# A gated linear recurrence and a two-layer network on one core: the decay sums' last rows turned by VectorE, the last output in two halves, another order of loads and work

## The chip, the cores and the metric

The kernel runs on one core of a Trainium2 chip. A core has five engines with a queue each: PE (TensorE, matmuls; its weight loads are shown apart as PEld), DVE (VectorE), ACT (ScalarE), POOL (GpSimd) and SP (SyncE, which issues the DMA transfers here). The engines work at the same time and wait for each other by semaphores. PSUM, into which PE writes, has eight banks of 128 partitions x 512 f32 values. The metric is device time in microseconds (us): the median of several executions, and beside it one execution that the hardware profiler recorded.

## The reference, cut to what matters

```python
# q, k, v, f_logit: (4 batches, 8 heads, 768 steps, 48), f32
f = 1.0 / (1.0 + np.exp(-f_logit))
for t in range(S):
    state = f[:, :, t, :, None] * state + np.einsum('bhd,bhe->bhde', k[:, :, t], v[:, :, t])
    y[:, :, t] = np.einsum('bhd,bhde->bhe', q[:, :, t], state)
x = y.transpose(0, 2, 1, 3).reshape(B * S, H * D)     # 3072 tokens x 384
h = x @ w_in                                          # 384 -> 2048
g = np.maximum(0.01 * h, h)
out = g @ w_out                                       # 2048 -> 384
```

Each head keeps a 48 x 48 state that decays with a gate for each of its rows; the outputs go through a two-layer network with a leaky relu.

## The kernel before

**Chunks.** The 768 steps are cut into six chunks of 128. Inside a chunk the recurrence is a masked product: with the running sum of -log f over the chunk, k is multiplied by exp(sum) and q by exp(-sum), the scores k q are masked to the lower triangle and multiplied with v. What came before the chunk enters through the state, and the state is carried to the chunk's end by a factor exp(-sum of the whole chunk), the tile `end`: one value for each row of each head's state, that is, for each pair of heads one column of 128 partitions (head one in partitions 0 to 47, head two in 64 to 111).

**Units.** Work comes in twelve units of 256 tokens. Units 0 to 3 are one batch each with its first two chunks ("paired"); units 4 to 11 are one chunk (2 to 5) of two batches. Since a chunk of a batch needs the state of the chunk before, unit 6 needs what unit 4 leaves, and so on.

**Steps.** The kernel is one long string, `order` (L537 to L602), whose words are run one after the other when the program is built. A word is a step, a unit, a half or group of it, an engine choice where there is one, and after "@" the PSUM banks that it writes. Each engine runs its own instructions in the string's order; the string therefore sets every queue. `manual_schedule` leaves this order as it is, and waits between engines are put in by the framework: where two engines touch one PSUM bank, the later one in the string waits for the earlier.

The steps of a unit, in the order in which data pass through them:
- Lf, Lk, Lq, Lv: loads, on SP (WI, WO: the pieces of the two weight matrices; w_in comes in two pieces of 256 columns and three of 512, w_out in four; cw casts a block of them to bf16 on the engine named last: 0 DVE, 1 ACT, 2 POOL).
- ge, gl (L231, L243): ACT makes log(1 + exp(-f_logit)).
- cs (L252 to L263): PE makes the running sums with a triangular matrix, one matmul of 384 columns for each half of units 4 to 11 (L260). In units 4 to 9 four matmuls of one column follow (L263): for a pair of heads p they multiply the pair's 128 columns with a column of ones, which gives the last row of the sums, turned into a column of 128 partitions.
- dec (L271, L272, L277): ACT takes exp(sum) into `em`, exp(-sum) into `at`, and of the four turned columns exp(-sum) into `end`.
- k, q (L283, DVE or POOL), v (L288 to L297, POOL): scaling and casts to bf16.
- tk, tq and ck, cq (L316, L331): transposes on PE and copies out of PSUM; in units 6 to 11 xk and xq, DMA transposes, instead.
- sc (L352, L359) scores, mk (L369, L373) masks on DVE, mx and ms (L390) the products with v and with the state, xt (L450, L452) the copy of x.
- pt (L463, L468) the chunk's k v, sf (L478, L480) its addition to the state on DVE, sb (L485, L488) the state's factor and its copy to bf16 on POOL.
- up (L496): the first layer for 256 of the 2048 inner values, 6 matmuls of 256 columns (eight groups for a unit); pr (L501): the leaky relu on ACT; dn (L508): a quarter of the second layer for 128 tokens, 4 matmuls of 384 columns; ob (L517 ACT, L519 DVE): the copy of the finished 128 x 384 outputs; st (L523): the store.
- id (L203): matmuls on constants that nothing reads, between the true ones at the start.

The first layer of a unit can start when x is there, so units' steps are laid between the up and dn groups of units before. The last words of the string are `dn_11_1_3 ob_11_0_1 st_11_0 ob_11_1_0 st_11_1`.

Of the kernel before, what the change touches and what calls it, by code (L numbers as in the profile page):

```python
# [15 lines left out]
def kernel(  # L16
# [228 lines left out]
    def cs(j, a, bank):  # L245
# [15 lines left out]
        if chunk(j, a) < NCH - 1:  # L261
            for p in range(P2):
                nc.tensor.matmul(t[:, H * D + p:H * D + p + 1], lf[:, a, 2 * p:2 * p + 2, :], ones_col,  # L263
                                 start=True, stop=True)
# [4 lines left out]
    def dec(j, a):
        t = banks[st[j]["cs", a]]  # L270
        nc.scalar.activation(ems[j % 2][:, a], t[:, 0:H * D], AF.Exp, scale=1.0)  # L271
        nc.scalar.activation(ats[j % 2][:, a], t[:, 0:H * D], AF.Exp, scale=-1.0)  # L272
        if paired(j):
            nc.scalar.activation(end_of(j)[:, :, 2 * a:2 * a + 2].rearrange("t i p -> t p i"),
                                 t[:, 384:388].rearrange("t (p i) -> t p i", i=2), AF.Exp, scale=-1.0)
        elif chunk(j, a) < NCH - 1:
            nc.scalar.activation(end_of(j)[:, a], t[:, H * D:H * D + P2], AF.Exp, scale=-1.0)  # L277
# [263 lines left out]
    id_8@2 sc_0_1@0.1 mk_0_0_1 mk_0_1_1 id_5@4 pt_0_2@2.3 WI_3 ge_1_0 mk_0_1_0 ge_1_1 gl_1_0 sf_0_0 id_8@6
    mx_0_2@4.5 gl_1_1 Lk_2_2 cs_1_0@6 sb_0_0 xt_0_0_1 cs_1_1@7 dec_1_0 WI_4 sf_0_1 ms_0 k_1_0_1 dec_1_1 q_1_0_0
    Lq_2_2 k_1_1_0 v_1_1 id_13@0 tk_1_0@1 xt_0_1_1 tq_1_0@0 q_1_1_0 tk_1_1@2 ck_1_0_1 v_1_0 cq_1_0_0 Lv_2_2
    tq_1_1@4 ck_1_1_1 sc_1_0@3.6 cq_1_1_0 cw_0_0_2 pt_1_2@7.5 mk_1_0_0 sc_1_1@1.0 sb_0_1 cw_0_1_0 up_0_0@2
    ge_2_0 mk_1_1_1 up_0_1@4 ge_2_1 mk_1_0_1 gl_2_0 pr_0_0 cs_2_0@3 mk_1_1_0 gl_2_1 sf_1_0 dec_2_0 cw_0_2_2
    mx_1_2@0.6 cw_0_3_0 cs_2_1@2 sb_1_0 pr_0_1 dec_2_1 xt_1_0_0 WO_0 id_5@7 up_0_2@1 sf_1_1 cw_0_4_2 cw_0_5_1
    up_0_3@7 sb_1_1 pr_0_2 ms_1 WO_1 up_0_5@3 pr_0_3 xt_1_1_0 Lf_3_2 up_0_4@4 k_2_0_0 Lk_3_2 k_2_1_1 pr_0_5
    up_1_2@0 pr_0_4 tk_2_1@2 pr_1_2 up_1_5@5 ck_2_1_1 cw_0_6_0 up_1_3@1 pr_1_5 tk_2_0@6 cw_0_7_0 pr_1_3 up_1_0@7
    ck_2_0_1 up_1_1@3 q_2_1_0 WO_2 pr_1_0 q_2_0_0 up_0_7@4 v_2_0 pr_1_1 tq_2_1@0 pr_0_7 tq_2_0@2 v_2_1 cq_2_1_0
    up_1_6@5 cq_2_0_1 sc_2_1@1.6 pr_1_6 cw_1_0_2 cw_1_1_0 sc_2_0@7.3 pt_2_2@4.0 up_1_4@2 mk_2_1_1 WO_3 mk_2_1_0  # L550
    Lq_3_2 dn_0_1_0@5 pr_1_4 Lv_3_2 mk_2_0_0 dn_0_0_0@6 cw_1_3_1 Lf_4_0 sf_2_0 up_1_7@1 Lk_4_0 ge_3_0 mk_2_0_1
    sb_2_0 up_0_6@2 ge_3_1 Lq_4_0 gl_3_0 cw_1_2_0 mx_2_2@7.4 gl_3_1 pr_0_6 cs_3_0@3 sf_2_1 Lv_4_0 xt_2_0_1 ms_2
    dn_0_1_1 sb_2_1 dec_3_0 k_3_0_0 dn_0_0_1 xt_2_1_1 pr_1_7 Lf_4_1 tk_3_0@2 cw_1_4_2 cw_1_5_0 up_2_6@0 up_2_4@7
    ck_3_0_0 pr_2_6 dn_0_1_2 pr_2_4 Lk_4_1 cw_1_6_2 cw_1_7_0 up_2_3@3 up_2_5@4 pr_2_3 Lq_4_1 q_3_0_1 up_2_7@1
    pr_2_5 up_2_0@2 Lv_4_1 v_3_0 pr_2_7 dn_0_0_2 pr_2_0 v_3_1 Lf_5_0 cs_3_1@0 dn_0_0_3 dec_3_1 Lk_5_0 up_2_1@7
    k_3_1_1 ob_0_0_0 Lq_5_0 up_2_2@3 pr_2_1 q_3_1_1 dn_1_1_0@4 pr_2_2 st_0_0 tk_3_1@1 tq_3_0@2 ck_3_1_0 tq_3_1@0
    Lv_5_0 ge_4_2 dn_0_1_3 cq_3_0_0 cq_3_1_0 sc_3_0@6.7 gl_4_2 ob_0_1_0 sc_3_1@3.1 pt_3_2@2.0 mk_3_0_1 Lf_5_1
    dn_2_1_0@5 mk_3_1_1 cs_4_0@7 mk_3_1_0 Lk_5_1 dn_1_1_1 dec_4_0 mk_3_0_0 cs_4_1@1 Lq_5_1 v_4_2 dn_1_1_2 sf_3_0
    dec_4_1 dn_2_1_1 k_4_2_0 Lv_5_1 sb_3_0 dn_1_1_3 q_4_2_0 Lf_6_0 dn_2_1_2 ob_1_1_1 sf_3_1 pt_4_0@3 tq_4_0@7
    Lk_6_0 tk_4_1@6 sf_4_0 dn_2_1_3 sb_3_1 Lq_6_0 ck_4_1_0 tk_4_0@2 cq_4_0_0 dn_1_0_0@1 Lv_6_0 ck_4_0_0 sb_4_0  # L560
    tq_4_1@4 dn_1_0_1 cq_4_1_1 Lf_6_1 mx_3_2@0.3 ge_5_2 sc_4_2@6.7.2.4 Lk_6_1 xt_3_0_0 gl_5_2 ms_3 mk_4_0_0
    dn_1_0_2 Lq_6_1 xt_3_1_0 cs_5_0@0 dn_1_0_3 mk_4_1_1 st_0_1 dec_5_0 v_5_2 mk_4_1_0 up_3_3@6 ob_1_0_1 mk_4_0_1
    cs_5_1@3 pr_3_3 up_3_1@4 st_1_0 dec_5_1 dn_2_0_0@0 k_5_2_1 pr_3_1 st_1_1 up_3_2@2 dn_2_0_1 pr_3_2 Lv_6_1
    q_5_2_1 up_3_4@1 Lf_7_0 pt_5_1@7 up_3_0@6 pr_3_4 sf_5_1 up_3_6@3 Lk_7_0 ge_6_2 sb_5_1 tq_5_1@4 pr_3_0
    tq_5_0@2 Lq_7_0 cq_5_1_0 up_3_5@1 gl_6_2 cq_5_0_0 dn_2_0_2 Lv_7_0 pr_3_6 cs_6_0@7 pr_3_5 Lf_7_1 cs_6_1@6
    ob_2_1_1 tk_5_0@4 Lk_7_1 tk_5_1@2 dec_6_1 ck_5_0_0 pt_5_0@3 st_2_1 dn_3_1_0@1 ck_5_1_0 sf_5_0 dec_6_0
    dn_2_0_3 Lq_7_1 v_6_2 dn_3_1_1 ob_2_0_1 Lv_7_1 pt_4_1@5 q_6_2_1 dn_3_0_0@4 sf_4_1 dn_3_1_2 Lf_8_0 dn_3_0_1
    sb_4_1 sc_5_2@2.6.3.7 st_2_0 mx_4_2@0.5 mk_5_0_0 k_6_2_1 mk_5_1_1 Lk_8_0 dn_3_0_2 xt_4_0_1 mk_5_0_1 xt_4_1_1
    up_3_7@2 xq_6 sb_5_0 ge_7_2 mk_5_1_0 up_4_2@7 pr_3_7 pt_6_1@0 xk_6 up_4_5@5 gl_7_2 sf_6_1 dn_3_0_3 pr_4_2
    sb_6_1 Lq_8_0 pr_4_5 dn_3_1_3 ob_3_0_0 Lv_8_0 pt_6_0@6 cs_7_0@3 ob_3_1_0 v_7_2 st_3_0 up_4_7@2 dec_7_0  # L570
    sf_6_0 up_4_6@0 Lf_8_1 sb_6_0 pr_4_7 Lk_8_1 up_4_0@7 pr_4_6 cs_7_1@5 pr_4_0 Lq_8_1 up_4_1@4 dec_7_1 up_4_4@1
    k_7_2_1 pr_4_1 up_4_3@6 pr_4_4 st_3_1 dn_4_1_0@3 pr_4_3 q_7_2_1 dn_4_0_0@2 pt_7_0@0 pt_7_1@7 dn_4_0_1 sf_7_0
    sf_7_1 mx_5_2@5.4 xk_7 sc_6_2@1.6.0.7 xt_5_0_1 sb_7_0 xq_7 dn_4_0_2 xt_5_1_1 mk_6_0_0 up_5_4@5 mk_6_0_1
    sb_7_1 Lv_8_1 dn_4_0_3 mk_6_1_1 pr_5_4 Lf_9_0 mk_6_1_0 up_5_6@4 ge_8_2 Lk_9_0 up_5_5@1 ob_4_0_1 Lq_9_0
    gl_8_2 up_5_0@6 pr_5_5 Lv_9_0 dn_4_1_1 pr_5_0 Lf_9_1 up_5_2@7 pr_5_6 up_5_7@5 pr_5_2 up_5_3@0 pr_5_7 Lk_9_1
    up_5_1@2 pr_5_3 dn_4_1_2 pr_5_1 cs_8_1@1 dn_5_1_0@6 Lq_9_1 dec_8_1 dn_4_1_3 dn_5_1_1 ob_4_1_0 Lv_9_1 v_8_2
    sc_7_2@4.7.5.0 dn_5_0_0@2 Lf_10_0 mk_7_0_0 dn_5_1_2 mk_7_1_1 st_4_1 dn_5_0_1 mk_7_0_1 mk_7_1_0 dn_5_1_3
    Lk_10_0 dn_5_0_2 ob_5_1_0 Lq_10_0 cs_8_0@1 dn_5_0_3 dec_8_0 Lv_10_0 mx_6_2@3.4 k_8_2_0 ge_9_2 q_8_2_1
    Lf_10_1 mx_7_2@0.7 ob_5_0_0 xt_6_0_1 xt_6_1_0 gl_9_2 pt_8_0@5 xk_8 xt_7_0_0 pt_8_1@6 up_6_4@1 xt_7_1_1
    sf_8_0 v_9_2 up_6_1@2 xq_8 pr_6_4 sf_8_1 up_6_2@3 pr_6_1 sb_8_0 up_6_0@4 Lk_10_1 pr_6_2 st_4_0 up_7_0@0  # L580
    pr_6_0 sb_8_1 Lq_10_1 cs_9_0@7 pr_7_0 dn_6_1_0@5 Lv_10_1 dec_9_0 up_6_3@1 up_6_6@6 pr_6_3 cs_9_1@2 st_5_0
    pr_6_6 up_6_5@3 dec_9_1 dn_6_1_1 st_5_1 k_9_2_1 pr_6_5 up_7_1@4 ge_10_2 up_7_4@0 pr_7_1 q_9_2_1 up_6_7@7
    xk_9 gl_10_2 pt_9_0@1 up_7_7@6 pr_6_7 sf_9_0 pr_7_4 dn_6_0_0@2 sb_9_0 xq_9 pr_7_7 up_7_5@3 dn_6_0_1 pr_7_5
    Lf_11_0 cs_10_1@4 up_7_6@7 Lk_11_0 dec_10_1 dn_6_1_2 Lq_11_0 pr_7_6 sc_8_2@1.0.6.3 Lv_11_0 v_10_2 dn_6_1_3
    mk_8_0_0 Lf_11_1 up_7_3@4 mk_8_0_1 Lk_11_1 ob_6_1_1 dn_6_0_2 mk_8_1_0 pr_7_3 mk_8_1_1 dn_7_0_0@7 dn_6_0_3
# [51 lines left out]
```

## Time and profile before

| | |
|---|---|
| median of 3 executions | 180.60 us (180.38 to 181.57) |
| profiled execution | 180.96 us |
| its span, first to last instruction | 179.0 us |
| granted clock of TensorE | 1.000 |
| read from and written to memory | 25.17 MB, 4.72 MB |

The page lists each engine's busy time with its share of the span, then 40 equal slices of the span (a digit is the busy share in tenths), the chain of work that ended last, and groups of instructions: line, engine, operation, output<-input, count, then busy us and mean ns of one, then the engine's idle us ahead of them with what ended it. The larger groups beside those that the prediction shows:

```profile
L496 PE MATMUL ps<-xT,w_in 128*128 128x256 bf16 x576 | 71.0, 273 | 1.0 <-issue 1.0
L508 PE MATMUL ps<-w_out,gT 128*128 128x384 bf16 x384 | 72.0, 326 | 0.0
...
L373 DVE TENSOR_TENSOR wm<-ps,ut 128x512 bf16<-128x512 f32 x32 | 20.0, 683 | 20.0 <-PE ps L359 12.2
...
L271 ACT ACTIVATE em<-ps 128x384 bf16<-128x384 f32 x24 | 11.9, 495 | 10.9 <-PE ps L263 7.3
```

The matmuls are pipelined, so a matmul's duration (273, 326 ns) holds its way through the array; from the start of one to the start of the next it is 109 ns for 256 columns and 162 ns for 384.

### The profile page before, as it was taken

The numbers are of one execution on the slowest core, as the hardware profiler recorded it, in microseconds if no ns is written. First come the engines' busy times: TensorE is split into PE (matmuls) and PEld (weight loads), VectorE is DVE, ScalarE is ACT, GpSimd is POOL, SyncE is SP. The second block draws the span as 40 slices with busy tenths as digits, with TensorE's granted clock in tenths as the row PEclk, the third lists the DMA queues.
The fourth block names the chain that finished last, engine by engine and source line by source line (L and its number), as shares of the span: only waits on it lengthen the run. The fifth ranks groups of instructions, "written<-read, shape, count | busy, mean of one in ns | idle before, by whom it ended". The sixth has DMA issues, their size and how long they took to land.

```text
span 179.0 us, 5623 instructions
## 1 busy us (share of the span) xinstructions
PE 171.8 (96%) x2326; PEld 130.9 (73%) x2326; DVE 81.4 (45%) x167; ACT 113.4 (63%) x234; POOL 74.4 (42%) x143
## 2 busy tenths in 40 slices
PE   7898979999999999999999999999999999999992
...
DVE  7878953961398714560711770142056065120001
...
GB/s 138 286 313 339 380 320 379 355 322 194 204 206 156 176 263 180 238 199 207 209 171 217 165 229 165 221 149 220 208 77 92 161 4 44 48 44 4 0 88 88
DMA packets 102105, 33.39 MB, mean 186 GB/s; under 512 B 96448, under 2 KB 100288, under 8 KB 102080
## 3 DMA queue, kind: packets, MB, share of 16 engines
...
q8 instruction: 18, 0.29, 0.6%
q14 instruction: 7, 0.06, 0.1%
HBM read 25.17 MB, written 4.72 MB: 167 GB/s over the span
## 4 chain that ended last, share of the span: by engine, by line
PE 87%; DVE 4%; DMA 2%; issue 2%; SPq 1%; POOL 1%; ACT 0%; DVEq 0%; ACTq 0%; POOLq 0%
PE ps L508 36%; PE ps L496 35%; PE ps L390 6%; DVE wm L369 3%; PE ps L359 2%; PE ps L316 2%; DMA q_raw<-in_q_dram 2%; PE ps L260 1%; SPq L154 1%; PE ps L468 1%; PE ps L352 1%; POOL qh L283 1%; PE ps L263 1%; PE ps L463 0%; DVE kh L283 0%
## 5 line engine op out<-in xcount | busy, mean ns | idle before, releaser
L496 PE MATMUL ps<-xT,w_in 128*128 128x256 bf16 x576 | 71.0, 273 | 1.0 <-issue 1.0
L508 PE MATMUL ps<-w_out,gT 128*128 128x384 bf16 x384 | 72.0, 326 | 0.0
L501 ACT ACTIVATE gT<-ps 128x512 bf16<-128x512 f32 x96 | 56.5, 603 | 20.6 <-PE ps L496 18.5
L496 PEld LDWEIGHTS <-w_in 128*128 128x128 bf16 x576 | 60.3, 110 | 6.8 <-issue 1.2
L508 PEld LDWEIGHTS <-gT 128*128 128x128 bf16 x384 | 35.7, 98 | 19.1
L373 DVE TENSOR_TENSOR wm<-ps,ut 128x512 bf16<-128x512 f32 x32 | 20.0, 683 | 20.0 <-PE ps L359 12.2
L519 DVE COPY osb<-ps 128x384 f32<-128x384 f32 x11 | 6.1, 557 | 35.7 <-PE ps L508 35.6
L480 DVE TENSOR_TENSOR sf<-sf,ps 64x192 f32<-64x192 f32 x32 | 11.2, 351 | 20.9 <-PE ps L468 8.5
L271 ACT ACTIVATE em<-ps 128x384 bf16<-128x384 f32 x24 | 11.9, 495 | 10.9 <-PE ps L263 7.3
L488 POOL CAST sb<-sf 64x192 bf16<-64x192 f32 x40 | 14.4, 361 | 10.0 <-DVE sf L478 7.7
L283 POOL TENSOR_TENSOR qh<-q_raw,at 128x768 bf16<-128x768 f32 (+1 forms) x9 | 13.6, 1509 | 10.8 <-ACT end L277 8.9
L283 POOL TENSOR_TENSOR kh<-k_raw,em 128x768 bf16<-128x768 f32 (+1 forms) x8 | 11.0, 1373 | 14.6 <-ACT em L271 11.2
L288 POOL CAST vb<-v_raw 128x384 bf16<-128x384 f32 (+1 forms) x16 | 11.3, 708 | 12.1 <-PE ps L496 4.7
L450 ACT CAST xT<-ps 128x384 bf16<-128x384 f32 x14 | 7.0, 526 | 11.4 <-PE ps L390 11.4
L517 ACT COPY osb<-ps 128x384 f32<-128x384 f32 x13 | 6.3, 482 | 11.5 <-PE ps L508 11.3
L231 ACT ACTIVATE e<-f_raw 128x384 f32<-128x384 f32 (+1 forms) x16 | 10.6, 684 | 2.4 <-DMA f_raw<-in_f_logit_dram 2.4
L272 ACT ACTIVATE at<-ps 128x384 bf16<-128x384 f32 x24 | 11.9, 497 | 0.0
L485 POOL TENSOR_TENSOR sf<-sf,end 128x192 f32<-128x192 f32 x16 | 8.4, 527 | 6.5 <-DVE sf L480 6.1
L243 ACT ACTIVATE lf<-e 128x384 bf16<-128x384 f32 (+1 forms) x16 | 10.7, 683 | 0.1
L369 DVE TENSOR_TENSOR wm<-ps,pair_mask 128x512 bf16<-128x512 f32 x16 | 10.1, 683 | 1.4 <-PE ps L352 1.3
L203 PE MATMUL ps<-warm 128*128 128x512 bf16 (+2 forms) x22 | 7.3, 452 | 1.1 <-DVE warm L82 1.1
L452 DVE CAST xT<-ps 128x384 bf16<-128x384 f32 x10 | 5.5, 568 | 4.9 <-PE ps L390 3.6
...
## 6 DMA issues: line engine op xcount, KB each, us to landing
...
```

Source lines behind the costliest of these rows:

```text
L271: nc.scalar.activation(ems[j % 2][:, a], t[:, 0:H * D], AF.Exp, scale=1.0)
L272: nc.scalar.activation(ats[j % 2][:, a], t[:, 0:H * D], AF.Exp, scale=-1.0)
L283: eng.tensor_mul(heads(j, to[j % NR], a)[:, :, :, 0:D], raw_heads(j, x, a), decays(j, by, a))
L288: nc.gpsimd.tensor_copy(out=heads(j, vb, a), in_=raw_heads(j, "v", a))
L369: nc.vector.tensor_mul(w.rearrange("t (s p) n -> t s p n", s=2), src.rearrange("t (s p n) -> t s p n", s=2, p=2), pair_mask[:, :, None, :] ...
L373: nc.vector.tensor_mul(w, src.rearrange("t (p n) -> t p n", p=P2), ut[:, None, :].to_broadcast([128, P2, 128]))
L390: nc.tensor.matmul(banks[st[j]["py", i]][32 * r:32 * r + 32, 128 * kk:128 * kk + 128], lhsT, rhs, start=(i, r) not in begun, stop=i in las ...
L480: nc.vector.tensor_add(sf[rows], sf[rows], new)
L488: nc.gpsimd.tensor_copy(out=sb[rows, :, y * D:y * D + D], in_=sf[rows])
L496: nc.tensor.matmul(pm[:, i, :], w_in_of(ff, kk), xTs[j % 3][:, kk].rearrange("t a s -> t (a s)"), start=(kk == 0), stop=(kk == NK - 1))
L501: nc.scalar.activation(gTs[j % 3][:, 2 * g:2 * g + 2, :], pm, AF.Prelu, alpha=0.01)
L508: nc.tensor.matmul(po, gTs[j % 3][:, ff, 128 * a:128 * a + 128], w_out_b[quarter][:, ff % 4, :], start=(ff == 0), stop=(ff == NF - 1))
```

## The change

Four things:
1. The one-column matmuls and the small activation behind each half (L263, L277) are gone in units 4 to 9. In their place `end_turn` (word et) has VectorE transpose blocks of 32 x 32 out of PSUM: partitions 96 to 127 of the sums, of which the last is the sums' last row, for each of four groups of 32 output partitions, the four head pairs side by side (32 partitions x 128 values for each of the four instructions). They go to the tile `es` of the unit, whose gate values are no longer needed then; its column 31 of each block is the row wanted. `end_exp` (en) takes exp(-x) of those columns for both halves in one activation of 112 x 8 values.
2. The last second layer, of unit 11's second half, is computed for columns 0 to 191 in 16 matmuls and then for 192 to 383 in 16 more (dh), in place of 16 of 384 columns. Each half is copied (oh: ACT the first, DVE the second) and stored (sh) by itself.
3. Loads: q of units 0 and 1 goes ahead of k; w_in's third piece is issued ahead of unit 1's v and the fourth behind it, the first two after them; unit 2's k, q, v ahead of the last piece; unit 3's f behind its v and q.
4. The whole string is another one. The first groups of the first layer are up_0_2 and up_0_3 (the third piece's columns) in place of up_0_0 and up_0_1; ACT casts 7 blocks of weights where it cast 2, DVE 3 where it cast 8, POOL 6 as before; steps, banks and engine choices (k, q, ck, cq, xt, ob) differ throughout.

```diff
         nc.tensor.matmul(t[:, 0:H * D], ut, lf[:, a, :, 0:D], start=True, stop=True)
-        if chunk(j, a) < NCH - 1:
-            for p in range(P2):
-                nc.tensor.matmul(t[:, H * D + p:H * D + p + 1], lf[:, a, 2 * p:2 * p + 2, :], ones_col,
-                                 start=True, stop=True)
...
-        elif chunk(j, a) < NCH - 1:
-            nc.scalar.activation(end_of(j)[:, a], t[:, H * D:H * D + P2], AF.Exp, scale=-1.0)
+
+    def last_row(j):
+
+        return es[j % 2][:, :, 0:32 * P2].rearrange("t a (p n) -> t a p n", p=P2)
+
+    def end_turn(j, a):
+        t, to = banks[st[j]["cs", a]], last_row(j)
+        for i in range(4):
+            lo = D * (i // 2) + 32 * (i % 2)
+            src = t[96:128, lo:lo + 2 * D * (P2 - 1) + 32]
+            src = bass.AP(tensor=src.tensor, offset=src.offset, ap=[src.ap[0], [2 * D, P2], [1, 32]])
+            nc.vector.transpose(out=to[32 * i:32 * i + 32, a], in_=src)
+
+    def end_exp(j):
+        rows = slice(0, 64 + D)
+        nc.scalar.activation(end_of(j)[rows], last_row(j)[rows, :, :, 31], AF.Exp, scale=-1.0)
...
+    def down_half(j, a, half, *bank):
+        if bank:
+            st[j]["po", a] = bank[0]
+        cols = slice(half * KD // 2, half * KD // 2 + KD // 2)
+        for ff in range(NF):
+            nc.tensor.matmul(banks[st[j]["po", a]][:, cols], gTs[j % 3][:, ff, 128 * a:128 * a + 128],
+                             w_out_b[ff // 4][:, ff % 4, cols], start=(ff == 0), stop=(ff == NF - 1))
+
+    def out_half(j, a, half, e):
+        cols = slice(half * KD // 2, half * KD // 2 + KD // 2)
+        src, dst = banks[st[j]["po", a]][:, cols], out_tile(j, a)[:, cols]
...
+    def store_half(j, a, half):
+        t = batch(j, a) * S + chunk(j, a) * C
+        cols = slice(half * KD // 2, half * KD // 2 + KD // 2)
+        nc.sync.dma_start(out=out[t:t + C, cols], in_=out_tile(j, a)[:, cols])
...
+        "et": end_turn, "en": end_exp, "dh": down_half, "oh": out_half, "sh": store_half,
```

Of the string, the loads' part and the places that the prediction speaks of, new ones, in its order ("..." where words are left out):

```
Lf_0_0 Lf_0_1 Lq_0_0 Lk_0_0 Lk_0_1 Lq_0_1 ... Lq_1_2 ... Lk_1_2 ... WI_2 Lv_1_2 ... WI_3 ... Lf_2_2 ... WI_0
... WI_1 ... Lk_2_2 ... Lq_2_2 ... Lv_2_2 ... WI_4 ... WO_0 ... Lk_3_2 ... WO_1 ... Lv_3_2 ... Lq_3_2 ... Lf_3_2
...
cs_4_0@4 cs_4_1@5 dn_1_0_2 dec_4_0 et_4_0 Lk_5_1 v_4_2 dn_0_0_2 dec_4_1 et_4_1 Lq_5_1 tk_3_0@7 dn_1_0_3 en_4
k_4_2_1 ck_3_0_1 Lv_5_1 dn_0_0_3 ob_1_0_1 sc_3_0@0.3
...
cs_7_1@7 dn_4_0_1 dec_7_1 et_7_1 mx_5_2@5.2 k_7_2_0 q_7_2_1 Lf_9_0 dn_4_0_2 xt_5_0_1 et_7_0 xt_5_1_1
pt_7_0@6 pt_7_1@4 dn_4_0_3 en_7
...
cs_8_0@5 cs_8_1@0 up_5_1@3 pr_5_7 et_8_0 dec_8_0 up_6_0@1 et_8_1 pr_5_1 up_6_1@6 dec_8_1
...
dn_10_0_3 up_11_5@2 ob_10_0_1 dn_11_0_1 st_10_0 pr_11_5 dn_10_1_0@3 dn_11_0_2 dn_10_1_1 dn_11_0_3 dn_10_1_2
ob_11_0_1 dh_11_1_0@5 st_11_0 dn_10_1_3 oh_11_1_0_1 sh_11_1_0 dh_11_1_1 ob_10_1_1 st_10_1 oh_11_1_1_0 sh_11_1_1
```

More of the change, by code (lines that the diff above doesn't have):

```diff
@@ L509, in down @@
                              start=(ff == 0), stop=(ff == NF - 1))
+    def down_half(j, a, half, *bank):
[8 more added lines that the diff above has]
+        src, dst = banks[st[j]["po", a]][:, cols], out_tile(j, a)[:, cols]
+        if e:
+            nc.scalar.copy(out=dst, in_=src)
+        else:
+            nc.vector.tensor_copy(out=dst, in_=src)
+    def store_half(j, a, half):
+        t = batch(j, a) * S + chunk(j, a) * C
+        cols = slice(half * KD // 2, half * KD // 2 + KD // 2)
+        nc.sync.dma_start(out=out[t:t + C, cols], in_=out_tile(j, a)[:, cols])
     def out_tile(j, a):
@@ L541 @@
[L541 to L585, printed above, removed]
@@ new lines @@
+    ob_1_1_0 pt_3_2@0.3 st_0_1 ck_3_1_1 dn_1_0_0@6 sf_3_0 ge_4_2 dn_0_0_0@1 sb_3_0 gl_4_2 tq_3_0@2 st_1_1
+    dn_0_0_1 sf_3_1 cq_3_0_1 dn_1_0_1 Lf_5_1 sb_3_1 cs_4_0@4 cs_4_1@5 dn_1_0_2 dec_4_0 et_4_0 Lk_5_1 v_4_2
+    dn_0_0_2 dec_4_1 et_4_1 Lq_5_1 tk_3_0@7 dn_1_0_3 en_4 k_4_2_1 ck_3_0_1 Lv_5_1 dn_0_0_3 ob_1_0_1 sc_3_0@0.3
+    Lf_6_0 ob_0_0_1 sc_3_1@2.4 q_4_2_1 mk_3_0_0 dn_2_0_0@5 mk_3_0_1 st_0_0 tk_4_1@7 pt_4_1@6 Lk_6_0 pt_4_0@1
+    mk_3_1_1 tk_4_0@0 dn_2_0_1 Lq_6_0 sf_4_1 tq_4_1@3 ck_4_0_0 dn_2_0_2 sb_4_1 cq_4_1_1 Lv_6_0 mk_3_1_0 tq_4_0@4
@@ new lines @@
+    up_5_5@1 ob_4_1_0 up_5_6@6 pr_5_5 mx_6_2@4.7 pr_5_6 st_4_1 up_5_7@2 xt_6_0_1 st_3_1 xt_6_1_1 cs_8_0@5
+    cs_8_1@0 up_5_1@3 pr_5_7 et_8_0 dec_8_0 up_6_0@1 et_8_1 pr_5_1 up_6_1@6 dec_8_1 up_6_2@4 Lk_9_1 k_8_2_1
+    pr_6_1 dn_5_1_0@7 pr_6_2 Lq_9_1 up_6_3@2 en_8 Lv_9_1 pr_6_0 q_8_2_1 up_6_7@5 pr_6_3 Lf_10_0 dn_6_1_0@3
+    pr_6_7 dn_5_1_1 xk_8 ge_9_2 sc_7_2@0.6.4.1 gl_9_2 dn_5_1_2 mk_7_0_0 xq_8 up_6_6@2 mk_7_0_1 dn_5_1_3 mk_7_1_0
+    Lk_10_0 pr_6_6 Lq_10_0 mk_7_1_1 up_6_5@5 ob_5_1_1 Lv_10_0 up_6_4@0 pr_6_5 Lf_10_1 dn_5_0_0@6 st_5_1 v_9_2
```

73 lines of the change are left out of this document (54 added, 19 removed).

## The prediction

> **What bounds the kernel now.** I read the page's head and busy slices first, then the chain of waits, then the groups by shape, then the timeline at the three places that the change touches.
>
> ```profile
> span 179.0 us, 5623 instructions
> ...
> PE 171.8 (96%) x2326; PEld 130.9 (73%) x2326; DVE 81.4 (45%) x167; ACT 113.4 (63%) x234; POOL 74.4 (42%) x143
> ...
> PE   7898979999999999999999999999999999999992
> ...
> DVE  7878953961398714560711770142056065120001
> ...
> PE 87%; DVE 4%; DMA 2%; issue 2%; SPq 1%; POOL 1%; ACT 0%; DVEq 0%; ACTq 0%; POOLq 0%
> ```
>
> PE is busy in every slice after the seventh until the last. The chain goes through PE for 87% of the span. VectorE is at 45% and has slices at 0 to 2. So after the start the time is PE's list of matmuls, one behind the other, and an edit counts by what it takes from this list or by a hole that it makes in it.
>
> ```profile
> 18.51 1.48 PE L496 MATMUL ps<-xT,w_in 128*128 128x256 bf16 x12
> ...
> 23.53 0.74 PE L496 MATMUL ps<-xT,w_in 128*128 128x256 bf16 x5 [1.02 <-issue]
> ```
>
> These rows of PE's timeline are the first first-layer matmuls and the last hole. Ahead of 23.5 us PE waits for loads, casts and masks; behind it I find no hole over 0.1 us except where the shape of the matmul tile switches (94 to 148 ns each, 5.1 us in 21 excursions).
>
> ```profile
> 50.89 0.33 PE L260 MATMUL ps<-lf,ut 128*128 128x384 bf16 x1
> 51.05 0.24 PE L263 MATMUL ps<-ones_col,lf 128*128 128x1 bf16 x4
> 51.16 0.81 PE L508 MATMUL ps<-w_out,gT 128*128 128x384 bf16 x4
> ```
>
> Start times, not durations, give the price in a pipelined list: the four one-column matmuls take from 51.05 to 51.16, 0.1 us.
>
> ```profile
> L480 DVE TENSOR_TENSOR sf<-sf,ps 64x192 f32<-64x192 f32 x32 | 11.2, 351 | 20.9 <-PE ps L468 8.5 <-ACT lf L243 8.3 <-issue 3.3
> ...
> L519 DVE COPY osb<-ps 128x384 f32<-128x384 f32 x11 | 6.1, 557 | 35.7 <-PE ps L508 35.6
> ...
> L263 PE MATMUL ps<-ones_col,lf 128*128 128x1 bf16 x48 | 2.9, 164 | 0.0
> ...
> L277 ACT ACTIVATE end<-ps 128x4 f32<-128x4 f32 x12 | 2.4, 198 | 0.0
> ```
>
> **One-column matmuls out.** In the groups by shape the first number is busy time, the second the mean of one in ns. Start to start over the whole trace one one-column matmul takes 25 ns, so 48 x 0.025 = 1.2 us leave PE's list. The matmul that follows is no shorter for it, so all of it is gain: -1.2. ScalarE loses 12 activations of 198 ns and gets 6; it has holes at those places, so I take 0.
>
> **VectorE's transposes in.** 48 of them, 32 partitions x 128 elements of f32 from PSUM, four to a half, writing partitions 0, 32, 64, 96 in turn. No row shows a transpose. The nearest by size: f32 reads from PSUM of 512, 384 and 192 elements take 683, 557 and 351 ns, 1.04 ns for an element, which gives 557 - 256 x 1.04 = 290 ns for 128. The question is whether one overlaps the next.
>
> ```profile
> 54.96 1.49 DVE L480 TENSOR_TENSOR sf<-sf,ps 64x192 f32<-64x192 f32 x4
> 56.47 0.42 DVE L331 COPY kT<-ps 128x512 bf16<-128x512 bf16 x1
> 56.81 0.41 DVE L331 COPY qT<-ps 128x512 bf16<-128x512 bf16 x1
> 57.15 0.41 DVE L331 COPY kT<-ps 128x512 bf16<-128x512 bf16 x1
> ```
>
> Full-height copies start 0.34 apart at 0.42 long, an overlap of 0.08. The state additions, which go to partitions 0 to 63 and 64 to 127 in turn, take 1.49 for four, 0.37 apart at 0.35 long: no overlap. Transposes change the start partition each time like the second, so I take 0.29 each (upper bound 0.30, with the additions' gap; lower bound 0.21, with the copies' overlap; a 128-element memset takes 0.165, and is the floor). The Trainium skill has a rule for this ("VectorE: DVE Perf Modes", section "Two Vector instructions with no wait between them"): an instruction whose input or output starts in another 32-partition quadrant than the last one's is held until the earlier ones have finished; by that rule, with which the two rows agree, the overlap is lost, and it speaks against this change. The same page ("The three transpose paths") gives 311 ns for a 128x128 bf16 transpose on VectorE; with it in place of 0.29 the sum below would be 0.7 us higher.
>
> 48 x 0.29 = 14 us on VectorE would lie beside PE, which has over 100 us left for it, but for one thing: a bank of sums is now read by two engines, and in the changed program as built their reads follow one another. Either the four transposes wait for ScalarE's two exponentials (units 4, 7, half of 5 and 9) or these wait for the transposes (6, 8, the other halves). So 4 x 0.29 = 1.2 us are put in series with the decays, which k, q, the transposes, the scores and the state wait for.
>
> Unit 4 worked out, from the end of its first sums: ScalarE's two exponentials start 386 and 370 ns apart, with 0.1 for a signal 0.87. Eight transposes in a row: 0.87 + 8 x 0.29 = 3.19 (the second half's exponentials end at 1.63 and are hidden). Then the small exponential (en_4, 0.2 and a signal 0.1), and behind it in ScalarE's queue the copy ck_3_0 (0.48 + 0.1), for which score sc_3_0 waits: 4.07. In that time PE has cs_4_1, 16 second-layer matmuls and 4 transposes: 0.16 + 16 x 0.162 + 4 x 0.056 = 2.98. PE stands for 1.1 us. In the same way, each from the PE work between sums and first reader at these starts (109 ns for a 256-column matmul), for 0.21 | 0.29 | 0.30 a transpose:
> - unit 4: 0.48 | 1.12 | 1.20
> - unit 5, second half, transposes ahead of the exponentials and k: 0.04 | 0.34 | 0.38
> - unit 6, transposes first in both halves; up_4_6 waits for its bank: 0.29 | 0.87 | 0.94
> - unit 7, k_7 behind the transposes on VectorE, then pt_7_0: 0.61 | 0.91 | 0.95
> - unit 8, ScalarE stands at dec_8_0 with pr_6_0 and pr_5_1 queued behind it, dn_5_1_0 and dn_6_1_0 late: 0.10 | 0.50 | 0.55
> - unit 9, first half, sf_8_1 and mx_7's copies behind the transposes, up_7_1 late: 0.40 | 0.69 | 0.73
> - unit 9, second half, transposes ahead of the exponentials and k_9: 0.04 | 0.40 | 0.44
>
> Sum 1.96 | 4.83 | 5.19. These holes are in a list with no slack, so I count them in full: +4.8.
>
> **Last second layer by halves.** 32 starts of 82 ns (192 columns, from the sums of the paired units) for 16 of 162: 2.62 for 2.60, nothing. Behind the last matmul the copy is half as wide, 351 for 557, -0.2 (row L480 is the only one of 192 columns). The last store, 96 KB for 192, went from issue 176.38 to landing 178.20: its change lies between 0 and half of 1.82 less; I take -0.1, since the same queue's median for the 192 KB stores is 3.0 and varies with what else runs more than with size. Together -0.3.
>
> **Loads.** Landings before, one 384 KB transfer about every 1.15 us and one 768 KB about every 2.05, the queue never empty until 42 us. w_in's third piece moves from 20.3 to about 14.9, the fourth from 22.4 to 18.2; unit 1's v falls from 13.9 to 16.3, unit 2's k, q, v come 1 to 3 us earlier, unit 3's v 8 earlier and f 2 later. The first first-layer groups are now those of pieces 2 and 3, ready before x is. Following each queue with starts as measured: the first score comes at 8.45 for 9.23 (in front of tq_0_1), unit 0's masks end 0.4 earlier, unit 1's about 1, first-layer matmuls start at 18.3 for 18.5, and the hole at 22.5 (1.02) is closed but for 0.2 where up_0_1 waits for ScalarE's cast. The 14th first-layer group ends at 32.8 for 33.7: -0.9. With full durations in place of start-to-start times on VectorE and GpSimd, it comes to +0.6; at best -1.6. ScalarE now casts seven blocks of weights at 0.73 apart in place of two; between 24 and 52 us it was busy 21.5 of 28, so 3.6 us more fit, and if not PE is next to wait.
>
> **Order.** The tile shape switches 3 times more into partial tiles, 4 times more out, 5 fewer between partial ones: +0.2. From 33 to 47 us and at the end (mx_10 and mx_11 next to each other) I find no hole.
>
> Sum: -1.2 + 4.8 - 0.3 - 0.9 + 0.2 = +2.6. The profiled execution took 180.96, 1.96 beyond its span; on the runs' median 180.6 that is 183.2.
>
> **Rivals.**
> 1. The transposes overlap like full-height copies (0.21): -2.2 + 1.96 = -0.3, so 180.3; down to 0.165 the holes shrink to about 0.75 and the time to 179.1. For it: all four read the same partitions, only the output moves. Against: the state additions' 0.37.
> 2. Faster: the holes don't open, because ScalarE's reads and the transposes interleave further ahead of PE than I walked it; then -1.2 - 0.3 - 0.9 + 0.2 = -2.2, 178.4. For it: a hole on PE lets the other engines get ahead, and VectorE is free about half of the time. It decides from 0.16 us a transpose down, or if unit 4 to 9's sums stand 1.2 us earlier beside PE's list than in my walk. Against: the decays were already read at once behind the sums (em's waits are for L263, 7.3 us of them).
> 3. The start is lost: ScalarE's casts or v of unit 1 hold the first-layer groups, +0.6 in place of -0.9: 184.7 with the held transposes.
> 4. The end rows' matmuls were hidden: not possible in a list without holes, so no chance of its own.
>
> **Numbers.** Forecast, held transposes: 0.44, own range 181.8 to 184.9 (start at its best -1.6 and transposes at 0.28, to the start lost). Rival 1: 0.26. Rival 2: 0.22. Rival 3: 0.08. The range goes from 178.2, just under rival 2, to 185.2. About 1% (178.8 and 182.4) is what a measurement of this kernel tells from no change. Faster: most of rival 2 (0.19) and the low end of rival 1 (0.06), 0.25. Within: 0.20 of rival 1, 0.03 of rival 2, 0.05 of the forecast's lower edge, 0.28. Slower: 0.47.
>
> **What would show it.** The transposes' row: mean near 290 ns, four of them 1.2 us from first to last; a span of 0.9 would be rival 1. PE's idle time in units 4 to 9 named after ScalarE or VectorE, at sc_3_0, pt_7_0 and up_7_1 first, 4 to 5 us of it; none would be rival 2. PE's rows 2301, without L263. First score near 8.45, first-layer matmuls at 18.3 without the 1.02 hole. Last copy near 0.35 and a last store that lands 1.7 to 1.8 after issue. I am wrong if PE shows no hole between 50 and 120 us, or if its holes lie before 35 us.

## The result, and the profile after

The changed kernel takes 188.04 us (187.66 to 188.45, 4 runs), the one before 180.97 (180.38 to 181.57, 4 runs): ratio 1.039 with a 95% interval of 1.034 to 1.044. The direction was forecast; the 7.1 us are 2.7 times the 2.6 forecast and lie above the range. The profiled execution took 188.35 with a span of 186.6, so the difference to the profile of before (180.96, 179.0) is 7.6 us of span.

The head of the page, PE's and VectorE's slices and the chain by engine, of the changed kernel:

```profile
span 186.6 us, 5623 instructions
...
PE 172.8 (93%) x2301; PEld 131.2 (70%) x2301; DVE 97.5 (52%) x210; ACT 117.5 (63%) x236; POOL 69.0 (37%) x141
...
PE   7897899999988998799799989799999999999993
DVE  7989647613457796836981543667653538000000
...
PE 58%; DVE 12%; DMA 8%; issue 7%; ACT 7%; SPq 4%; POOL 3%; DVEq 0%; ACTq 0%; POOLq 0%
```

The change did what it says: 2301 matmuls in place of 2326, 16 us more on VectorE. But PE's slices now have sevens and eights in the middle, and the chain goes through PE for 58% in place of 87%, with more of it on VectorE, ScalarE and DMA. By stages (columns: window in us, its length, busy us of PE, PEld, DVE, ACT, POOL with instruction counts, granted clock, DMA share, GB/s), before and after:

```profile
52.00:125.00 73.00, 73.00 (x1004) 56.87 (x1003) 32.59 (x68) 48.61 (x107) 39.39 (x61) 1.00 1.04 197
```

```profile
52.00:125.00 73.00, 66.16 (x877) 50.45 (x876) 45.99 (x107) 46.81 (x96) 31.74 (x52) 1.00 0.95 187
```

PE loses 6.8 us of busy time of 73 in the stretch in which units 4 to 9 make their sums; in the kernel before it loses none there. From start to start of matmuls (each gap less its kind's usual one and the 0.09 to 0.15 of a tile switch) the holes there sum to 8.1 us. They stand where the prediction put them, and are larger. (The third column carries the prediction's figures on from 0.29 to 0.345 us a transpose at their own slope, 0.36 us of holes for 10 ns.)

| hole | predicted at 0.29 us a transpose | the same at 0.345 | measured |
|---|---|---|---|
| unit 4, ahead of sc_3_0 | 1.12 | 1.56 | 1.52 |
| unit 5, ahead of tk_5_0 | 0.34 | 0.56 | 1.07 |
| unit 6, at up_4_4 and up_4_6 | 0.87 | 1.26 | 1.38 |
| unit 7, ahead of pt_7_0, and ahead of dn_4_1_0 | 0.91 | 1.12 | 1.37 + 0.28 |
| unit 8, ahead of dn_5_1_0 | 0.50 | 0.78 | 0.71 |
| unit 9, ahead of up_7_1 | 0.69 | 0.90 | 1.25 |
| unit 9, ahead of pt_9_1 | 0.40 | 0.64 | 0.54 |
| sum | 4.83 | 6.82 | 8.12 |

Unit 4's, in the timeline of the changed kernel (start, length, engine, line, what; in brackets idle time ahead and its releaser):

```profile
53.03 2.73 DVE L283 STREAM_TRANSPOSE e<-ps 32x128 f32<-32x128 f32 x8 [2.32 <-ACT at L268]
...
53.62 1.46 PE L518 MATMUL ps<-w_out,gT 128*128 128x384 bf16 x8
55.79 0.21 ACT L287 ACTIVATE end<-e 112x8 f32<-112x8 f32 x1 [2.02 <-DVE e L283]
55.91 0.57 ACT L339 COPY kT<-ps 128x512 bf16<-128x512 bf16 x1
...
56.53 0.47 PE L362 MATMUL ps<-qT,kT 48*64 48x128 bf16 x20 [1.46 <-ACT kT L339]
```

Eight transposes take 2.73 us in a row, ScalarE stands 2.02 us at the small activation that wants the last of them, the copy of kT stands behind it in ScalarE's queue, and PE waits 1.46 us for that copy. A transpose takes 320 ns, not 290, and the next starts 0.330 to 0.355 us after it, 0.345 in the mean. `end_turn`'s row is:

```profile
L283 DVE STREAM_TRANSPOSE e<-ps 32x128 f32<-32x128 f32 x48 | 15.4, 320 | 11.8 <-ACT at L268 6.7 <-PE ps L260 4.1
```

### The profile page after: what moved, and what is told of

It is laid out like the page before. It is cut to its first block, busy times and chain, and to the rows that moved or that the text cites. A ratio compares the mean times of both kernels' runs of the same rounds, so it can differ in the third digit from the quotient of the medians.

```text
span 186.6 us, 5623 instructions
## 1 busy us (share of the span) xinstructions
PE 172.8 (93%) x2301; PEld 131.2 (70%) x2301; DVE 97.5 (52%) x210; ACT 117.5 (63%) x236; POOL 69.0 (37%) x141
## 4 chain that ended last, share of the span: by engine, by line
PE 58%; DVE 12%; DMA 8%; issue 7%; ACT 7%; SPq 4%; POOL 3%; DVEq 0%; ACTq 0%; POOLq 0%
PE ps L518 24%; PE ps L506 21%; DVE e L283 6%; DMA v_raw<-in_v_dram 4%; PE ps L400 4%; DVE kh L293 3%; SPq L158 3%; DMA k_raw<-in_k_dram 2%; ACT em L267 2%; PE ps L369 2%; ACT gT L511 2%; DMA out_dram<-osb 2%; ACT at L268 1%; PE ps L526 1%; PE ps L326 1%
## 5 line engine op out<-in xcount | busy, mean ns | idle before, releaser
L511 ACT ACTIVATE gT<-ps 128x512 bf16<-128x512 f32 x96 | 55.7, 605 | 23.9 <-PE ps L506 22.1
L518 PE MATMUL ps<-w_out,gT 128*128 128x384 bf16 x368 | 69.5, 326 | 0.9 <-ACT gT L511 0.5
L518 PEld LDWEIGHTS <-gT 128*128 128x128 bf16 x368 | 34.4, 98 | 20.3 <-ACT gT L511 1.0
L283 DVE STREAM_TRANSPOSE e<-ps 32x128 f32<-32x128 f32 x48 | 15.4, 320 | 11.8 <-ACT at L268 6.7
L293 POOL TENSOR_TENSOR qh<-q_raw,at 128x384 bf16<-128x384 f32 (+1 forms) x10 | 14.0, 1408 | 17.1 <-ACT at L268 10.9
L498 POOL CAST sb<-sf 64x192 bf16<-64x192 f32 x40 | 13.6, 341 | 4.0 <-DVE sf L488 1.7
L293 DVE TENSOR_TENSOR kh<-k_raw,em 128x384 bf16<-128x384 f32 (+1 forms) x11 | 9.2, 844 | 4.0 <-ACT em L267 2.4
L293 POOL TENSOR_TENSOR kh<-k_raw,em 128x768 bf16<-128x768 f32 (+1 forms) x5 | 6.7, 1347 | 10.9 <-ACT em L267 10.9
L550 DVE COPY osb<-ps 128x384 f32<-128x384 f32 x9 | 5.0, 557 | 10.9 <-PE ps L518 10.9
```

The lines of the kernel that those rows point to most:

```text
L283: nc.vector.transpose(out=to[32 * i:32 * i + 32, a], in_=src)
L293: eng.tensor_mul(heads(j, to[j % NR], a)[:, :, :, 0:D], raw_heads(j, x, a), decays(j, by, a))
L498: nc.gpsimd.tensor_copy(out=sb[rows, :, y * D:y * D + D], in_=sf[rows])
L511: nc.scalar.activation(gTs[j % 3][:, 2 * g:2 * g + 2, :], pm, AF.Prelu, alpha=0.01)
L518: nc.tensor.matmul(po, gTs[j % 3][:, ff, 128 * a:128 * a + 128], w_out_b[quarter][:, ff % 4, :], start=(ff == 0), stop=(ff == NF - 1))
```

## The experiments

Twelve kernels. Ratios are to the kernel before on the same chip, with 95% intervals. **Theory A** at the start: the transposes, in series with ScalarE's reads of the same bank, make the holes. **Theory B**: the new order makes them.

**e1, all matmuls back.** The change's order, loads and halves, without the transposes:

```diff
+        if chunk(j, a) < NCH - 1:
+            for p in range(P2):
+                nc.tensor.matmul(t[:, H * D + p:H * D + p + 1], lf[:, a, 2 * p:2 * p + 2, :], ones_col, ...
...
+        elif chunk(j, a) < NCH - 1:
+            nc.scalar.activation(end_of(j)[:, a], t[:, H * D:H * D + P2], AF.Exp, scale=-1.0)
...
-    et_j_a, en_j   # all 18 words out of the order
```

> The changed kernel with its order, loads and last halves, but the sums' last rows again by the four one-column matmuls and the small activation of before; no transposes. Theory A (the transposes, in series with the decays' reads of the same bank, make the holes on PE between 52 and 122 us, 8.2 us of them by the gaps between starts): the holes go, the matmuls cost 48 x 25 ns = 1.2, so 188.0 - 8.2 + 1.2 = 181.0, between 180.4 and 181.6, and PE has no hole over 0.2 us behind 52 us. Theory B (the new order itself, with its other engines for k, q, casts and copies, makes them): the holes stay, 188 to 189.

181.19 us, ratio 1.0008 (0.9986 to 1.0030). PE is busy for the whole of the stretch:

```profile
52.00:125.00 73.00, 73.00 (x1029) 56.41 (x1028) 36.38 (x69) 51.12 (x110) 36.31 (x58) 1.00 1.00 204
```

Theory B falls: the order without the transposes has no hole there. The whole loss comes with the transposes. Everything else in the change together is worth nothing that can be measured.

**e2, one transpose of four; e3, eight.**

```diff
-        for i in range(4):
+        for i in range(1):                        # e2
+        for i in (0, 1, 2, 3, 0, 1, 2, 3):        # e3
```

> The changed kernel with the first of each half's four transposes alone; the factors of three quarters of the state's rows are then left out (stale values stand there). Waits and their order stay. Theory A with the duration as the cost (4 x 0.345 us in series): about 0.36 us of holes for each 10 ns of a transpose, so at a quarter nearly none is left: 180 to 181. Theory A' (not the duration but the handing over of the bank from one engine to the other costs): most of the holes stay, 185 to 187.5. Theory B: 187.5 to 188.

> The changed kernel with each half's four transposes done twice. Theory A: 1.38 us more in series in each of 12 halves, 16.6 us at most, some 12 by the slopes of the prediction's table: 197 to 203. Theory A': 188 to 191. Theory B: VectorE has half of its time free, 188 to 190.

e2, which leaves out the factors of three quarters of the state's rows: 181.44 us, ratio 1.002 (0.998 to 1.006). The wait from engine to engine is still there, so it isn't the handing over that costs (theory A'), it is the time that the transposes take. One hole stayed, at pt_7_0, as long as before (1.37), and with it the time is a little above the 180 to 181 expected; of that more under e10. e3: 212.45 us, 1.174 (1.168 to 1.180), 24.4 more than with four, where 9 to 15 was expected and 16.6 called the most. The holes grew by some 16 us, close to that bound: with eight, next to nothing of the added transposes is hidden. The rest goes with a cost that neither theory had named: the granted clock of PE fell, and behind 50 us the matmuls outside the holes take 7 us longer from start to start than in the changed kernel.

```profile
52.00:90.00 38.00, 26.31 (x357) 19.28 (x355) 27.99 (x73) 16.06 (x34) 13.83 (x23) 0.90 0.71 154
90.00:125.00 35.00, 29.98 (x335) 22.07 (x334) 21.28 (x54) 17.59 (x35) 10.54 (x18) 0.92 0.82 144
...
PEclk9999999999957999958999999987999999999999
```

In these two windows of e3 the third figure from the end, the clock, is 0.90 and 0.92. The last line is the clock in the page's 40 slices, in tenths: the longest hole, 4.5 us from 54.9 on, lies at the slice with a 5 (57.6 to 62.9 us). In the changed kernel itself, with holes up to 1.5 us, the clock stayed at 1.00 in this stretch.

**e4, exponentials first everywhere.**

```diff
-    et_5_1 dec_5_1    et_6_1 dec_6_1    et_6_0 dec_6_0    et_8_0 dec_8_0    et_9_1 dec_9_1
+    dec_5_1 et_5_1    dec_6_1 et_6_1    dec_6_0 et_6_0    dec_8_0 et_8_0    dec_9_1 et_9_1
-    et_8_1 pr_5_1 up_6_1@6 dec_8_1
+    pr_5_1 up_6_1@6 dec_8_1 et_8_1
```

> The changed kernel with the two exponentials ahead of the transposes also where the order has the transposes first (unit 5's second half, both of 6, both of 8, unit 9's second). Theory A, the place in series counts: the exponentials no longer wait for 1.4 us, the holes at 70.7, 77.3, 107.1 and 121.7 us (3.5 us together) shrink to 1 or less: 185 to 186. Rival: what follows the transposes in VectorE's queue (k of the unit, copies) is as late either way, and the holes stay: 187.5 to 188.5.

189.04 us, ratio 1.044 (1.041 to 1.047): no gain over the changed kernel, where theory A expected 185 to 186. Unit 5 in e4, and k there in the changed kernel:

```profile
69.49 1.37 DVE L283 STREAM_TRANSPOSE e<-ps 32x128 f32<-32x128 f32 x4 [0.78 <-ACT at L268]
...
70.89 1.10 DVE L293 TENSOR_TENSOR kh<-k_raw,em 128x768 bf16<-128x768 f32 x1
```

```profile
70.85 0.96 DVE L293 TENSOR_TENSOR kh<-k_raw,em 128x768 bf16<-128x768 f32 x1 [0.62 <-ACT em L267]
```

The exponentials no longer wait, but VectorE itself now makes the transposes ahead of unit 5's k, which begins at 70.89; in the changed kernel, with the exponentials behind the transposes, it begins at 70.85. Unit 8's hole did go (0.71 to 0.2), where k is GpSimd's; those of 5, 6 and 9 did not. So the price is what stands behind the transposes, whichever engine reads the bank first (**theory C**). In units 5, 7 and 9 that is a k or a copy in VectorE's own queue; in unit 4 it is the copy of kT behind the small activation in ScalarE's. Unit 6 is a case of its own: its group up_4_6 wants the bank of the sums itself, and so waits for both readers in either order. In the changed kernel it waits for the last exponential:

```profile
78.48 0.49 PE L506 MATMUL ps<-xT,w_in 128*128 128x256 bf16 x3 [1.00 <-ACT at L268]
```

In e4 the same matmul starts at 78.91, behind 1.01 us of waiting for the last transpose.

**e5, transposes in the old order.** Kernel before, `et_j_a` put right behind `dec_j_a`, `en_j` ahead of the unit's first sb, matmuls out.

> The kernel before, order and all, but with the transposes in place of the one-column matmuls: each half's four right behind its two exponentials, the small activation for both halves ahead of the unit's first sb. Theory C (the price is what stands behind the transposes in VectorE's queue, and behind the small activation in ScalarE's, not the order that they were put into): holes of the same kind, 4 to 10 us, less 1.2 for the matmuls: 184 to 190. Rival (the changed order has lost slack that the old order has; VectorE is idle for more than half of the time): 179.7 to 181.

189.04 us, ratio 1.042 (1.038 to 1.045), holes of 8.2 us between 54 and 113 us, the longest 2.76 at unit 4's state, which waits for k behind the second half's transposes. The transposes leave 8 us of holes in either order.

**e7, the transposes late.** Matmuls for three halves in which the bank is wanted again too soon; the other nine behind what PE waits for:

```diff
+    MATMUL = ((6, 0), (6, 1), (7, 0))
-    ... et_5_1 dec_5_1 st_2_0 up_3_4@3 k_5_2_0 en_5 ...
+    ... dec_5_1 st_2_0 up_3_4@3 k_5_2_0 et_5_1 ... pr_3_7 en_5 ...
-    ... et_7_1 mx_5_2@5.2 k_7_2_0 ...          et_9_0 Lk_10_1 mx_7_2@1.7 sf_8_1 ... xt_7_1_0 ...
+    ... mx_5_2@5.2 k_7_2_0 et_7_1 ...          Lk_10_1 mx_7_2@1.7 sf_8_1 ... xt_7_1_0 et_9_0 ...
```

> The changed kernel with matmuls for both halves of unit 6 and the first of 7, and the transposes of the other nine halves moved behind what the path waits for: behind k of the unit in 5 and 7, behind q in 9's second half, behind mx_7's copies in 9's first, behind the exponentials in 8; each small activation some words later in ScalarE's queue. Theory C: the holes behind 52 us go, 36 of 48 matmuls stay away (-0.9 against the kernel with all matmuls back, 181.19 there, ratio 1.0008): 180.2 to 181, ratio 0.995 to 1.000. Rival (14 us more on VectorE cost their time wherever they are): 185 to 188.

181.32 us, ratio 1.0017 (0.9988 to 1.0045), just above the 0.995 to 1.000 expected. Unit 5 in e7, and the stretch:

```profile
68.63 0.96 DVE L302 TENSOR_TENSOR kh<-k_raw,em 128x768 bf16<-128x768 f32 x1 [0.40 <-ACT em L273]
69.62 1.38 DVE L291 STREAM_TRANSPOSE e<-ps 32x128 f32<-32x128 f32 x4
71.03 0.42 DVE L350 COPY kT<-ps 128x512 bf16<-128x512 bf16 x1
```

```profile
52.00:125.00 73.00, 72.34 (x998) 55.30 (x996) 47.20 (x104) 50.92 (x105) 36.80 (x59) 1.00 0.99 204
```

VectorE is busy for as long as in the changed kernel (47.2 us of the 73, there 46.0), and PE gets 72.34 of 73. The holes sum to 1.4 us where the changed kernel had 8.1. Unit 6's 1.4 and the 0.3 ahead of dn_4_1_0 went with the matmuls of the three halves. The rest, some 6.5, shrank to 1.4 with 36 of the 48 transposes still there, since little on the path waits behind them. Theory C holds; its rival (VectorE's load as such) falls. But these holes (0.3 to 0.4 at 55.7, 56.5, 70.7 and 116.9 us) give back the 0.9 of the matmuls left out.

**e13, transposes at seven halves**, matmuls also for (4, 1) and (9, 1).

> The kernel of e7_turns_late with matmuls also for unit 4's and 9's second halves, where small holes stood (0.32 and 0.36 at 55.7 and 56.5 us, 0.39 at 116.9): transposes at seven halves. Theory C: these holes go, 28 of 48 matmuls stay away (0.7 us) against the kernel with all matmuls back (ratio 1.0008): 0.997 to 0.999. Rival (what VectorE does more comes back in other waits): 1.001 or more.

180.87 us, ratio 0.9990 (0.9961 to 1.0019). The size lies as expected, but the interval holds e1's ratio and 1 too: that the transposes can gain anything is not shown.

**e6, the same four reads, written to the same partitions.**

```diff
-            nc.vector.transpose(out=to[32 * i:32 * i + 32, a], in_=src)
+            nc.vector.transpose(out=es[j % 2][0:32, a, 128 * (0, 1, 2, 1)[i]: ... + 128] ..., in_=src)
```

> The changed kernel with all four transposes of a half written to partitions 0 to 31, at other columns; the factors of three quarters of the state's rows are left out. Theory H (a transpose is held until the one before is done because its output starts at another partition): start to start 0.25 us or less in place of 0.33 to 0.35, four in about 1.05 in place of 1.35, the time 185 to 186.5. Rival (transposes never overlap): 0.33 to 0.35 as before, 187.5 to 188.5.

The eight of unit 4, which took 2.73 us, in e6:

```profile
54.31 1.79 DVE L283 STREAM_TRANSPOSE e<-ps 32x128 f32<-32x128 f32 x8 [2.32 <-ACT at L268]
```

Start to start it is mostly 0.211 us at 275 ns long, for 0.330 to 0.355 at 320; the time is 183.96 us (two runs; ratio 1.016, 1.012 to 1.020), below the 185 to 186.5 expected. Theory H holds, at the prediction's lower bound of 0.21. The Trainium skill ("VectorE: DVE Perf Modes", section "Two Vector instructions with no wait between them") says that an instruction whose output starts in another quadrant (32 partitions) than the last one's is held until the earlier ones have finished. These two traces, whose transposes differ in where they write and in nothing else, agree: being held costs 0.12 to 0.14 us for each transpose.

**e10, e2 with unit 7's q on VectorE.**

```diff
-    q_7_2_1
+    q_7_2_0
```

> The kernel of e2_one_turn (one transpose for a half, three quarters of the state's factors left out) with unit 7's q on VectorE, behind its k, in place of GpSimd. There the hole ahead of pt_7_0 stood at 1.37 us as with four transposes, while VectorE's k took 2.25 us beside GpSimd's q; with matmuls, where k began first, it took 0.96 and q 2.03 in place of 1.64. Theory P (the two engines' scalings exclude each other: the one that begins second waits until the first is done): k takes 0.8 to 1.0, the hole goes, 181.4 - 1.3 = 180.1. Rival (k is slow there for another reason): 2 us and more, the hole stays, 181.4.

The two scalings of unit 7 in e1 (matmuls; k begins first), in e2 (one transpose ahead of k) and in e10:

```profile
84.68 0.96 DVE L299 TENSOR_TENSOR kh<-k_raw,em 128x768 bf16<-128x768 f32 x1 [0.56 <-ACT em L271]
...
85.11 2.03 POOL L299 TENSOR_TENSOR qh<-q_raw,at 128x768 bf16<-128x768 f32 x1 [3.38 <-ACT end L277]
```

```profile
84.57 1.64 POOL L293 TENSOR_TENSOR qh<-q_raw,at 128x768 bf16<-128x768 f32 x1 [3.30 <-ACT at L268]
...
84.78 2.25 DVE L293 TENSOR_TENSOR kh<-k_raw,em 128x768 bf16<-128x768 f32 x1
```

```profile
84.91 0.91 DVE L293 TENSOR_TENSOR kh<-k_raw,em 128x768 bf16<-128x768 f32 x1
```

In e2 GpSimd's q ends at 84.57 + 1.64 = 86.21, and VectorE's k, begun at 84.78, ends 0.82 behind that. In e1 it is GpSimd's that is stretched, by 0.39. In e10 k takes 0.91 and the hole at pt_7_0 is gone: 180.85 us, ratio 0.998 (0.995 to 1.000) for e2's 1.002, half the gain that was expected, with intervals that overlap. So the trace shows the hole go, and the time alone would not show it. Whichever begins second is held up.

In the changed kernel this adds little. Its k of unit 7:

```profile
90.14 1.10 DVE L293 TENSOR_TENSOR kh<-k_raw,em 128x768 bf16<-128x768 f32 x1
```

It begins right behind the transposes, when GpSimd's q (88.79 to 90.43) is nearly done, and takes 0.2 us more than alone: the rest of the delay is the transposes' own. With four transposes and with one, k ends 0.8 us behind q, which fits the hole of 1.37 us in both.

**e9 and e11, the end alone,** on the kernel before:

```diff
-    ... dn_11_1_0@5 dn_11_0_1 dn_11_1_1 dn_11_0_2 dn_11_1_2 dn_11_0_3 dn_11_1_3 ob_11_0_1 st_11_0 ob_11_1_0 st_11_1
+    ... dn_11_0_1 dn_11_0_2 dn_11_0_3 ob_11_0_1 st_11_0 dh_11_1_0@5 oh_11_1_0_1 sh_11_1_0 dh_11_1_1 oh_11_1_1_0 sh_11_1_1
+    (e11: dh_11_1_1@6)
```

> The kernel before with nothing changed but the last second layer by two column halves (its first half's quarters now all ahead of it), with half copies and half stores. The prediction's term: 0.2 from the copy and 0.1 from the store, ratio 0.998; if the last store's time doesn't hang on its size, 0.9985 to 0.999; rival: the half stores interfere, 1.000 or more.

> The kernel of e9_old_order_halves with the second column half in another PSUM bank. There PE stood 0.57 us between the halves, until ScalarE had copied the first half out of the bank that they share. Expected: no hole there, and the prediction's term of the end, 0.3 to 0.35 less than before: ratio 0.998. Rival (the end hangs on the number of stores, not on their size): 1.000.

e9: ratio 1.0015 (0.9994 to 1.0035), because of a wait that the edit itself made:

```profile
175.07 1.48 PE L516 MATMUL ps<-w_out,gT 128*128 128x192 bf16 x16 [0.41 <-ACT osb L523]
```

The second half wants the bank that ScalarE copies the first half out of. The changed kernel has a quarter of another half (dn_10_1_3) in between and no such wait. e11, with two banks: 180.67 us, ratio 0.9972 (0.9948 to 0.9995). The half copy takes 0.36 for 0.56, and a 96 KB store lands 1.60 after its issue where one of 192 KB takes 1.82: 0.4 us. e11 is the one version here whose interval lies below 1, by little.

**e12, ten short fills at the start,** for the hole at 22 us:

```diff
+    id_1@6 x10
     Lf_0_0 Lf_0_1 Lk_0_0 ...
```

> The kernel before with ten more matmuls of 128 columns that nothing reads at the very start, where PE waits for loads anyway. In all kernels so far with a hole at 22.2 to 22.7 us, it stood behind PE's 350th or 351st matmul (704 or 705 instructions with the weight loads), whatever that matmul was. Theory F (PE's instructions themselves come late there): the hole stands again behind the 350th or 351st matmul, which is now ten matmuls earlier in the work, near 21.2 us. Rival (a weight cast or x comes late): it stays at the same matmul of the work, now the 361st, near 22.2 us. The time is that of before within 0.5 us either way.

The hole in e12, and in the changed kernel:

```profile
21.26 0.26 PE L252 MATMUL ps<-lf,bu 128*128 128x192 bf16 x1
22.82 0.24 PE L253 MATMUL ps<-lf,bs 128*128 128x192 bf16 x1 [1.30 <-issue]
```

```profile
23.20 0.49 PE L506 MATMUL ps<-xT,w_in 128*128 128x256 bf16 x3 [0.61 <-issue]
```

It went with the count: again behind PE's 351st matmul, now amid unit 2's sums, ten matmuls earlier in the work. Ratio 1.0009 (0.9986 to 1.0031). The traces show what else goes with it. A 16 KB packet of the DMA queue that the page lists as q8, instruction, lands at 21.2 to 22.3 us in the eleven traces with the hole, and in each of them the hole ends 1.26 to 1.52 us behind that landing. Of the three without it, e3 and e10 start the same matmul 1.30 and 1.36 us behind the landing, and in e13, where the packet lands at 20.0, PE comes to it only at 22.3. No run moved the packet alone.

## Why the prediction was wrong

The step that failed is the term of the transposes, a size: +4.8 us of holes were forecast and 8.1 measured. Second come the start and the order, +0.2 measured for -0.7 forecast. Together with the end (-0.4 for -0.3) that is 4.1 of the 4.5 us between the forecast +2.6 and the measured 7.1; the rest lies within the measurement's interval.

- **One-column matmuls, -1.2.** Not measured alone. The balance of e1 to the changed kernel (188.04 - 181.19 = 6.85, against holes of 8.1 less 1.2) agrees.
- **Transposes, +4.8: the mis-sized term.** Place and order of the holes were right; their sum was 8.1. Of the 3.3 missing, 2.0 are the transpose itself, 0.345 us from start to start for 0.29: 0.03 of it is its length (320 ns for 290), 0.025 the gap behind it. The length was taken from VectorE's longer reads of PSUM, in 64 and 128 partitions (1.04 ns an element). The upper bound of 0.30 took the state additions' gap as 0.013. That was misread: the four shown start 0.379, 0.390 and 0.359 us apart at 0.35 long, so two of their three gaps are 0.03. With it the bound would have been 0.32, still short, since no row showed a transpose's length. The remaining 1.3 are in single holes: unit 5 (0.51 above the third column), unit 9's first (0.35), unit 7's two (0.25 and 0.28) and unit 6 (0.12), with units 4 and 8 and unit 9's second 0.04 to 0.10 below it. In unit 7, 0.2 is k held by GpSimd's q, and the 0.28 is an output copy on VectorE behind the second transposes, for whose bank dn_4_1_0 waits. In unit 5 the rows show a chain in which each step pays its length, 0.5 for the exponential and 1.0 for k, where exponentials in a row start 0.386 apart. That is read from rows, not from a run, and the rest stays open.
- **The two engines' reads one behind the other.** That the bank's two readers are put in series, ahead of everything that waits for the decays, was given as the cause. e4 shows that their order matters in unit 8 alone. Elsewhere the cause is what stands behind the transposes (theory C), which the prediction's walks had in them, but not in its reason.
- **Rivals.** Rival 1 (transposes that overlap) falls with the 0.345; e6 shows that overlap only with the output partitions left the same. Its sum, -2.2 + 1.96, is -0.24 and not -0.3. Rival 2 (the holes don't open) is refuted for this order and for the old one (e5); in e7 and e13, with other places for the words and matmuls at three and five halves, most of them don't. Rival 3 (the start lost, +0.6) is not what happened: see next.
- **Start -0.9 and order +0.2.** PE's time without work (fills, holes, switches) is 0.2 us longer in e1 than before: +0.2 in place of -0.7. In the changed kernel the first score came at 8.47 (8.45 forecast) and unit 0's masks ended 0.54 earlier (0.4). But first-layer matmuls began at 18.71 (18.3 forecast, 18.51 before), and unit 1's masks ended 0.55 earlier and not 1. The hole at 22.5, which was to be closed but for 0.2, stayed at 0.6 to 0.8 in the changed kernel and e1: it had been read as a wait for a weight cast, and it is none (e12). By the prediction's own mark, the end of the 14th first-layer group, the new order is some 0.35 ahead and not 0.9: 33.4 us is the median of nine traces with it (32.9 to 34.1), 33.75 that of five with the old order (33.6 to 34.0). By these medians some 0.55 was lost behind that mark, for 0.2 forecast, of which a hole of 0.27 at 45.7 us in e1 is one piece; the traces spread too widely to share it out further.
- **End, -0.3.** Right: -0.4 in the rows (copy 0.2, store 0.2), ratio 0.997 in e11.
